# Narrower first weight loads and earlier transposes in the opening of a gated-MLP and long-convolution kernel

## The chip, the cores and the metric

The kernel runs on one core of a Trainium2 chip. The metric is the device time of one execution in microseconds; the median of three runs is given. A profiled execution is a run of its own, with its own time, and its trace covers a span that is a little shorter than that time.

## What is computed

The input `A_q` has 2048 rows of 640 columns. It is layer-normalised to `xn`, and two branches are added to it:

```python
xn  = layernorm(x)                                   # x = A_q, 2048 x 640
A   = xn * (causal long convolution of (shift_conv(k) * v) with ssm_k, plus D term)
B   = (sigmoid(xn @ w_gate) * (xn @ w_up)) @ w_down  # 640 -> 1728 -> 640
out = x + A + B
```

The change touches only the beginning of branch B: the first load of `x` and of the two weights, and the first products with them.

## The kernel before

**Layout.** The 2048 rows are 16 blocks of 128 (`b` in `x[:, b, :]`; row 16p+b lies on partition p). Four blocks make a tile `t` of 512 rows. For each tile `xn` is transposed block by block on TensorE (`xn_mm`, L230, five 128x128 transposes into `pt`), copied to `xnT` (`xn_ev`, L236; ScalarE's copy has L223), and multiplied with 128 columns of a weight at a time. Such a product is five matmuls of 512 columns (`product`, L253, matmuls at L257), one for each 128 of the 640 rows of the weight. ScalarE takes the sigmoid of the gate product (`gate_ev`, L266), and VectorE multiplies it with the up product into `hT` (`up_ev`, L272). The down product (L296) follows, and VectorE adds it to `x` (L301).

Both weights lie in one tile `w`, gate columns first, up columns from `UP` on. `load_w(eng, lo, hi, u)` loads columns lo to hi of gate (u = 0, DMA at L173) or up (u = 1, L176), as 5 chunks on 128 partitions.

**The opening.** Tile 0 starts before all its rows are there. For the first two column groups (fc = 0 and 1) its products are made in quarters: `quarter(u, fc, i)` (L242, matmuls at L248) multiplies one block of 128 rows. `turn(i)` (L484) transposes block i and copies it. The order on TensorE is 15 matmuls on zeros (`busy`, L482), turn 0, two more such matmuls, then block after block the four quarters gate 0, up 0, gate 1, up 1, with the turns in between: turn 1 after up 0 of block 0, turn 2 after up 0 of block 1, turn 3 after up 1 of block 1.

Behind each block of `x` stands a chain on VectorE: statistics (`ln_stats`, L198, two halves), aggregation (L202), variance (L210), then a power on GpSimd (L214) and the normalised block (`ln_xn`, L219). The chain of the next block is interleaved with it.

**What sets the order.** Everything is scheduled by hand. Each engine executes its instructions in the order in which the program issues them, and after the opening that order is the string ORDER (L621), one letter for each step. DMAs are issued from two queues only: SyncE's (SP) for nearly all of them, and ScalarE's (ACT) for three at the very beginning. In a queue they are issued in program order. After the loads shown in the diff, SyncE's queue goes on with the weight columns from 512 up, `w_down`, k (`load_k`, L155, first read by VectorE at L329), `ssm_k` (L139) and v (L169).

**Buffers.** The transposed blocks of tile 0 and `idle` share two PSUM buffers (`psC`), and the gate and up products have four (`psG`). A fifth product waits until the first of these is read: the first whole product takes the buffer that the sigmoid of gate 0 frees.

Of the kernel before, what the change touches and what calls it, by code (L numbers as in the profile page):

```python
# [19 lines left out]
P = 128  # L20
# [37 lines left out]
def kernel(  # L58
# [14 lines left out]
    nc = tc.nc  # L73
    xr = A_q.flatten_outer_dims().rearrange("(p b) d -> p b d", b=NB)
# [30 lines left out]
    x = res.tile([P, NB, DM], BF16, name="x")  # L105
# [15 lines left out]
    sync = nc.sync  # L121
# [49 lines left out]
    def load_w(eng, lo, hi, u):  # L171
        if u == 0:
            eng.dma_start(w[:, :, lo:hi], wgr[:, :, lo:hi])  # L173
            return
        h = min(hi, 13 * P)
        eng.dma_start(w[:, :, UP + lo:UP + h], wur[:, :, lo:h])  # L176
        if hi == FF:
            eng.dma_start(w[:, :, FF:UP], wur[:, :, h:FF])
# [51 lines left out]
    def xn_mm(g, i):  # L230
        pool, tag = (psG, "g") if g else (psC, "c")
        xts[i] = pt = pool.tile([P, NC, P], BF16, name="pt", tag=tag)
        for c in range(NC):
            nc.tensor.transpose(pt[:, c, :], xn[:, 4 * g + i, c * P:(c + 1) * P], ident[:])  # L234

    def xn_ev(g, i, copy=act_copy):  # L236
        copy(out=xnT[:, i, :, :], in_=xts[i][:, :, :])
# [4 lines left out]
    def quarter(u, fc, i):  # L242

        if i == 0:
            pgs[u, fc] = psG.tile([P, 512], F32, name=("pg", "pu")[u], tag="g")
        o = u * UP + fc * P
        for c in range(NC):
            nc.tensor.matmul(pgs[u, fc][:, i * P:(i + 1) * P], lhsT=w[:, c, o:o + P], rhs=xnT[:, i, c, :],  # L248
                             start=(c == 0), stop=(c == NC - 1))
# [216 lines left out]
        nc.vector.tensor_tensor(xs, xs, chunks[c]["yx", m][:, :, :], ALU.add)  # L466


    sync.dma_start(x[:, 0, :], xr[:, 0, :])
    nc.scalar.dma_start(x[:, 1, :], xr[:, 1, :])  # L470
    nc.scalar.dma_start(x[:, 2:4, :], xr[:, 2:4, :])
    for u in range(2):
        load_w((sync, nc.scalar)[u], 0, 256, u)
    for u in range(2):
        load_w(sync, 256, 512, u)

# [7 lines left out]
    def turn(i):  # L484
        xn_mm(0, i)
        xn_ev(0, i)
# [13 lines left out]
    for i in range(4):  # L500
        for fc in range(2):
            for u in range(2):
                quarter(u, fc, i)
            if (i, fc) in ((0, 0), (1, 0), (1, 1)):
                turn(1 + i + fc)
    for fc in range(2):
        gate_ev(0, fc)
        up_ev(0, fc)
# [158 lines left out]
```

## Time and profile before

| what | us |
|---|---|
| median of 3 runs (lowest, highest) | 239.71 (239.46, 240.14) |
| the profiled execution's own time | 239.41 |
| its span in the trace | 237.6 |
| TensorE (PE) busy | 231.4 |
| VectorE (DVE) busy | 190.3 |
| ScalarE (ACT) busy | 141.2 |
| first whole product (L257) starts | 14.34 |
| last matmuls end | 234.4 |
| x block 0, issue to landing | 3.2 |
| x blocks 2 and 3, issue to landing | 4.4 |
| first up load on ScalarE's queue, issue to landing | 7.1 |

All times inside the execution count from the start of the span. PE is the matmul part of TensorE and PEld its weight loads, which overlap with it; DVE is VectorE, ACT ScalarE, POOL GpSimd and SP SyncE. A matmul's shown length includes its way through the array, so that neighbours overlap: the distance from start to start is what one costs in a row of them. "Idle before <- releaser" names what ended a wait. A DMA's line shows its issue; its data come later, at its landing. The DMA view counts packets: one packet is one contiguous row piece, so a weight load of 256 columns (2 bytes each) has packets of 512 bytes and one of 128 columns has packets of 256.

### The profile page before, as it was taken

To read this page: it belongs to the slowest core of one execution; us is meant where nothing else is said; L and a number is where in the kernel's file an instruction comes from. 1 tells how busy PE (TensorE), PEld (TensorE's weight loads), DVE (VectorE), ACT (ScalarE), POOL (GpSimd) and SP (SyncE) were. 2 spreads that over 40 slices of the span, in tenths; PEclk is the share of its full clock that TensorE was granted. 3 is DMA by queue.
4 is the path that set the end of the run, shared out by engine and by line. 5 is a ranking of instruction groups with operands and counts; after the bars stand their busy time and mean duration, and the time that the engine had idled before them with its cause. 6 is when DMAs were issued, how large, how long until landed. Compare 5 with 4: busy or idle time off the path is not lost.

```text
span 237.6 us, 5553 instructions
## 1 busy us (share of the span) xinstructions
PE 231.4 (97%) x2265; PEld 135.1 (57%) x2265; DVE 190.3 (80%) x350; ACT 141.2 (59%) x178; POOL 11.2 (5%) x24
## 2 busy tenths in 40 slices
PE   8799999999999999999999999999999999999994
PEld 2564445878556455667754434577664434456782
DVE  3633889999999999999999999865585695968372
ACT  2342331728559897864888887997558858764000
POOL 4210000020000000002001000000000000000000
PEclk9999999999999999999999999999999999999999
DMA  7999999889998999999444888975939795285674
GB/s 212 292 314 233 259 322 298 183 249 284 253 311 243 253 295 297 284 267 319 148 183 152 234 230 258 227 228 203 241 109 222 186 281 123 89 238 144 196 237 134
DMA packets 88975, 54.82 MB, mean 231 GB/s; under 512 B 47670, under 2 KB 83062, under 8 KB 88694
## 3 DMA queue, kind: packets, MB, share of 16 engines
q1 hardware_dynamic: 88006, 53.66, 80.8%
q10 hardware_dynamic: 944, 0.82, 1.1%
q8 instruction: 17, 0.28, 0.5%
q14 instruction: 8, 0.07, 0.1%
HBM read 36.12 MB, written 18.35 MB: 229 GB/s over the span
## 4 chain that ended last, share of the span: by engine, by line
PE 95%; DMA 3%; ACT 0%; DVE 0%; ACTq 0%; issue 0%
PE pd L296 26%; PE pg L257 23%; PE pu L257 23%; PE psb L456 4%; PE ps L357 4%; PE ps L355 4%; PE ps L388 3%; DMA w<-in_B_w_up_dram 3%; PE psa L417 2%; PE pg L278 2%; PE pt L234 2%; PE pu L248 1%; PE pg L248 1%; ACT xnT L223 0%; DVE x L301 0%; ACT L119 0%
## 5 line engine op out<-in xcount | busy, mean ns | idle before, releaser
L257 PEld LDWEIGHTS <-w 128*128 128x128 bf16 x500 | 46.5, 98 | 54.3 <-issue 5.3
L296 PE MATMUL pd<-wd,hT 128*128 128x320 bf16 x448 | 64.3, 299 | 0.0
L257 PE MATMUL pg<-xnT,w 128*128 128x512 bf16 x250 | 62.2, 379 | 0.0
L257 PE MATMUL pu<-xnT,w 128*128 128x512 bf16 x250 | 62.1, 379 | 0.0
L296 PEld LDWEIGHTS <-hT 128*128 128x128 bf16 x448 | 42.8, 98 | 17.8 <-issue 1.7
L266 ACT ACTIVATE sig<-pg 128x512 bf16<-128x512 f32 x52 | 31.3, 605 | 30.1 <-PE pg L257 28.2
L272 DVE TENSOR_TENSOR hT<-sig,pu 128x512 bf16<-128x512 bf16 x52 | 35.2, 679 | 14.7 <-PE pu L257 9.3
L223 ACT CAST t<-ps 128x1024 bf16<-128x1024 f32 x40 | 39.1, 1023 | 11.4 <-DMA d<-t 6.3
L223 ACT CAST xz<-ps 128x1024 bf16<-128x1024 f32 x40 | 38.6, 1018 | 10.6 <-PE ps L388 10.5
L301 DVE TENSOR_TENSOR x<-pd,x 128x320 bf16<-128x320 f32 x32 | 15.4, 480 | 15.8 <-PE pd L296 15.7
L403 DVE TENSOR_TENSOR xz<-xz 128x2048 bf16<-128x2048 bf16 x20 | 24.4, 1220 | 0.2
L357 PE MATMUL ps<-kvh,S1t 128*128 128x128 bf16 x160 | 21.2, 219 | 0.0
L335 DVE TENSOR_TENSOR acc<-acc,tmp 128x1024 bf16<-128x1024 bf16 x30 | 20.7, 689 | 0.7
L355 PE MATMUL ps<-kvh,S1t 128*128 128x128 bf16 x160 | 21.2, 217 | 0.0
L333 DVE TENSOR_TENSOR tmp<-kx,sc 128x1024 bf16<-128x1024 bf16 x30 | 20.6, 687 | 0.4
L223 ACT CAST ao<-psa 128x1024 bf16<-128x1024 f32 x16 | 15.6, 1014 | 5.6 <-PE psa L417 3.5
L461 DVE TENSOR_TENSOR yx<-psb,xn 128x512 bf16<-128x512 f32 x20 | 13.8, 691 | 3.9 <-PE psb L456 2.9
L355 PEld LDWEIGHTS <-S1t 128*128 128x128 bf16 x160 | 15.5, 97 | 2.3
L357 PEld LDWEIGHTS <-S1t 128*128 128x128 bf16 x160 | 15.3, 96 | 2.3
L223 ACT COPY xnT<-pt 128x640 bf16<-128x640 bf16 x16 | 10.2, 709 | 10.8 <-PE pt L234 10.5
L198 DVE BATCH_NORM_STATS2 st<-x 128x6 f32<-128x320 bf16 x32 | 13.7, 471 | 2.8 <-DMA x<-in_A_q_dram 2.8
L401 DVE STREAM_SHUFFLE xz<-xz 128x512 f32<-128x512 f32 x20 | 14.6, 728 | 0.0
(44 smaller groups left out, 146.1 us busy)
## 6 DMA issues: line engine op xcount, KB each, us to landing
d<-t SPq DMA_DIRECT2D x20, 512.0 KB, 3.7
t<-d SPq DMA_DIRECT2D x20, 512.0 KB, 4.9
bi<-d SPq DMA_DIRECT2D x8, 512.0 KB, 5.5
d<-ao SPq DMA_DIRECT2D x6, 512.0 KB, 4.1
kx<-in_A_k_dram SPq DMA_DIRECT2D x10, 256.0 KB, 5.0
hn<-in_A_ssm_k_dram SPq DMA_DIRECT2D x20, 128.0 KB, 6.0
kvh<-in_A_v_dram SPq DMA_DIRECT2D x10, 256.0 KB, 5.2
x<-in_A_q_dram SPq DMA_DIRECT2D x3, 640.0 KB
```

Of the source, the lines that this page charges most:

```text
L223: nc.scalar.copy(out=out, in_=in_)
L257: nc.tensor.matmul(pg[:, :], lhsT=w[:, c, u * UP + fc * P:u * UP + (fc + 1) * P], rhs=xnT[:, :, c, :], start=(c == 0), stop=(c == NC - 1))
L266: nc.scalar.activation(sig[fc][:, :], pgs[0, fc][:, :], ACT.Sigmoid)
L272: nc.vector.tensor_tensor(hT[:, fc, :], sig[fc][:, :], pgs[1, fc][:, :], ALU.mult)
L296: nc.tensor.matmul(pd[:, :], lhsT=hT[:, fc, bb * P:(bb + 1) * P], rhs=wd[:, fc, 320 * half:320 * half + 320], start=(fc == 0), stop=(fc == ...
L301: nc.vector.tensor_tensor(x[:, 4 * t + bb, es], pds[bb, half][:, :], x[:, 4 * t + bb, es], ALU.add)
L333: nc.vector.tensor_tensor(d["tmp"][:, :, :], kx[:, lo + 3 - m:hi + 3 - m, :], sb(m), ALU.mult)
L335: nc.vector.tensor_tensor(d["acc"][:, :, :], d["acc"][:, :, :], d["tmp"][:, :, :], ALU.add)
L355: nc.tensor.matmul(ps[:, i, 0:P], lhsT=S1[:, b, h, :], rhs=cin[c]["kvh"][:, 0, b, :], start=True, stop=True)
L357: nc.tensor.matmul(ps[:, i, P:2 * P], lhsT=S1[:, b, h, :], rhs=hp[:, b // 2, b % 2, :], start=True, stop=True)
L401: nc.vector.stream_shuffle(z[:, 2, :, :].bitcast(F32), z[:, 1, :, :].bitcast(F32), swap)
L403: nc.vector.tensor_tensor(z[:, 1:3, :, :], z[:, 0:1, :, :].to_broadcast((P, 2, 8, P)), z[:, 1:3, :, :], ALU.mult)
```

## The change

```diff
-    sync.dma_start(x[:, 0, :], xr[:, 0, :])
-    nc.scalar.dma_start(x[:, 1, :], xr[:, 1, :])
-    nc.scalar.dma_start(x[:, 2:4, :], xr[:, 2:4, :])
-    for u in range(2):
-        load_w((sync, nc.scalar)[u], 0, 256, u)
+    for n in range(2):
+        for i in range(2):
+            (sync, nc.scalar)[i].dma_start(x[:, 2 * n + i, :], xr[:, 2 * n + i, :])
+        for u in range(2):
+            load_w((sync, nc.scalar)[u * (1 - n)], P * n, P * n + P, u)
     for u in range(2):
         load_w(sync, 256, 512, u)
...
         for fc in range(2):
             for u in range(2):
                 quarter(u, fc, i)
-            if (i, fc) in ((0, 0), (1, 0), (1, 1)):
-                turn(1 + i + fc)
+                if u + fc == 0 and i < 3:
+                    turn(i + 1)
```

The loads: columns 0 to 256 of both weights were one load of 320 KB each, gate on SyncE's queue, up on ScalarE's. Now they are four loads of 160 KB. Blocks 2 and 3 of `x`, one load of 320 KB on ScalarE's queue before, become two of 160 KB. The queues now carry, in order:

| queue | before | after |
|---|---|---|
| SP | x0, gate 0:256, gate 256:512, up 256:512, ... | x0, gate 0:128, x2, gate 128:256, up 128:256, gate 256:512, up 256:512, ... |
| ACT | x1, x2 and x3, up 0:256 | x1, up 0:128, x3 |

The turns: the turn of block i+1 now stands behind gate 0 of block i, for blocks 0, 1 and 2. The quarters keep their order, the instructions on the compute engines are the same in number and kind, and ORDER and everything after the opening stays as it is.

## The prediction

> **What bounds the kernel.** The first view is the busy time of each engine, and beside it the waits of the PE queue:
>
> ```profile
> PE 231.4 (97%) x2265; PEld 135.1 (57%) x2265; DVE 190.3 (80%) x350; ACT 141.2 (59%) x178; POOL 11.2 (5%) x24
> ```
> ```profile
> PE idle L482 <- DVE hT L117: 1.2, 1, 1.2
> PE pu L248 <- DMA w<-in_B_w_up_dram: 0.6, 1, 0.6
> PE pt L234 <- DVE xn L219: 0.6, 1, 0.6
> PE pg L248 <- ACT xnT L223: 0.6, 2, 0.3
> ```
>
> PE is busy for 231.4 of 237.6 us. All its waits that the second view names lie in the opening, before the loop over ORDER starts. The busy time by stage says the same (stretch in us, its length, then busy time of PE, PEld and so on, granted clock, DMA share, GB/s):
>
> ```profile
> 7.78:14.34 6.56, 5.74 (x95) 5.39 (x95) 2.31 (x10) 2.72 (x5) 1.74 (x3) 1.00 1.17 291
> 14.34:40.00 25.66, 25.66 (x125) 11.87 (x123) 18.49 (x28) 7.66 (x13) 0.42 (x1) 1.00 1.12 282
> 40.00:160.00 120.00, 120.00 (x1208) 72.70 (x1206) 115.24 (x213) 89.16 (x112) 5.41 (x7) 1.00 0.85 247
> 160.00:234.40 74.40, 74.36 (x823) 42.90 (x820) 49.80 (x89) 39.45 (x48) 0.00 (x0) 1.00 0.67 187
> ```
>
> From 14.34 us, the first whole product (L257), to 234.40 PE idles 0.04 us. So what the change does to the start of that product goes through to the end unless something that does not move with PE becomes late. The quarters' stage is the one to read, line by line in the timeline (start, length, engine, line; a bracket holds idle time and its releaser):
>
> ```profile
> 7.03 0.69 ACT L223 COPY xnT<-pt 128x640 bf16<-128x640 bf16 x1 [4.37 <-PE pt L234]
> 7.50 0.43 DVE L219 TENSOR_SCALAR xn<-x,mv,rstd 128x640 bf16<-128x640 bf16 x1
> 7.78 0.44 PE L248 MATMUL pg<-xnT,w 128*128 128x128 bf16 x5 [0.35 <-ACT xnT L223]
> 8.81 0.45 PE L248 MATMUL pu<-xnT,w 128*128 128x128 bf16 x5 [0.60 <-DMA w<-in_B_w_up_dram]
> 9.10 0.44 PE L234 MATMUL pt<-ident,xn 128*128 128x128 bf16 x5
> 9.58 0.69 ACT L223 COPY xnT<-pt 128x640 bf16<-128x640 bf16 x1 [1.85 <-PE pt L234]
> 10.32 0.44 PE L248 MATMUL pg<-xnT,w 128*128 128x128 bf16 x5 [0.22 <-ACT xnT L223]
> ```
>
> Groups of five matmuls follow one another every 0.28 us where nothing waits (12.10, 12.38, 12.66). From 7.78 to 14.34 stand 16 quarters and 3 turns: 19 x 0.28 = 5.32 of 6.56 us. The other 1.24 are waits, counted by starts: 8.06 to 8.81 for the up weights (0.75), 9.94 to 10.32 for xnT of block 1 (0.38), 12.00 to 12.10 for block 2 (0.10).
>
> **Part 1, the order on PE.** No instruction is added or removed on PE, ACT or DVE. A turn costs the group that needs it 1.22 us from its own start: 0.48 to the copy (9.10 to 9.58), 0.69 copy, 0.05 to the matmul (10.27 to 10.32); 10.88 to 12.10 is the same 1.22. Now the turn of block i+1 stands behind the first gate group of block i, and three other groups (0.84) follow it before block i+1 begins. Turn and cover make 1.12, so 0.10 stays as a wait, and one block takes 0.28 + 1.22 = 1.50 us. The first gate groups start at 7.78 (unchanged: xnT of block 0 sets it, and the chain of x block 0, its statistics and turn(0) is not touched), 9.28, 10.78 and 12.28. From the gate group of block 3 to the first product it is 1.13 now (13.21 to 14.34; sig of L266 frees the PSUM buffer at 14.29) and the four groups of block 3 keep their order, so that product starts at 13.41: **0.93 us earlier**.
>
> What is late next? The turns go up to xn. Turn 1 would stand at 8.06, and xn of block 1 is there at 7.93 + 0.05: 0.08 to spare. Turn 2 at 9.56 against 9.43, turn 3 at 11.06 against 10.85. What queues behind a turn that waits is every quarter after it. This holds if DVE's rows stay, so x blocks 2 and 3 must land by 6.71 and 8.16, where their statistics (L198) start, block 2 by 6.79 with the spare 0.08.
>
> **Part 2, the loads.** The trace has no 128-column weight load. Its price comes from the DMA view of two microseconds, the first (20 to 21 us) with loads of 256-byte rows of k, the second (8.2 to 9.2 us) with 512-byte rows of weights:
>
> ```profile
> DMA packets 857, 0.22 MB, mean 224 GB/s; under 512 B 848, under 2 KB 857, under 8 KB 857
> ```
> ```profile
> DMA packets 579, 0.29 MB, mean 289 GB/s; under 512 B 14, under 2 KB 579, under 8 KB 579
> ```
>
> A weight load is 640 packets (128 partitions, 5 chunks) whatever its width: 640/579 = 1.11 us at 256 columns, 640/857 = 0.75 at 128. Four narrow loads take 3.0 us of the DMA engines where two wide ones took 2.2: 0.2 more each. Lower end: half a wide load, nothing more. Upper end: a narrow packet as dear as a wide one, 0.55 more each. I take 0.2, the row of the same packet size.
>
> When do they land? The rates by microsecond (19, 212, 367, 372, 303, 293 GB/s from 1 to 7 us) add up to 970 kB at 5.0 us and 1273 kB at 6.0. Up to x block 2 the new order moves at most four blocks of x and two narrow loads, 983 kB (5.05 us); up to the second up load 1311 kB (6.1 us). Add 0.4 and 0.8 for small packets: 5.45 and 6.9. Then the lag to landing: x blocks 2 and 3 landed at 1.22 + 4.4 = 5.6 while their equal share of two queues was through at 5.05, 0.55; the up load on ScalarE's queue landed at 1.65 + 7.12 = 8.77 where that share says 7.25, 1.5. I take 0.55 for x (its own row) and keep both for the weights. Block 2 lands near **6.0** (needed 6.79), the second up load at **7.5 to 8.4** (its group now starts at 8.90, and 0.10 more is covered by the wait for xnT). The first up half has less ahead of it, and needs 8.34. So the 0.75 wait goes, and no DMA takes its place.
>
> The Trainium skill speaks against this change: "DMA: Bandwidth & Descriptors", Specifications, wants transfers of 512 bytes or more for line rate and says that shorter ones are read, modified and written. If that made a narrow packet as dear as a wide one, the gain would shrink to that of rival B. The trace agrees in direction only: 224 against 289 GB/s, not half.
>
> On SyncE's queue stand three more issues, 0.4 to 0.5 each. The waits of that queue name one for an x block, 0.3 before the ninth transfer (L176 at 4.17). In the new order the ninth is gate 256:512, so I let it move from 1.64 to about 4.2. With the slowest early landing, 7.1, it is there at 11.3; needed at 13.41. All loads behind come 0.8 later, PE 0.93 earlier. The tightest is k's first half (L155, issued 15.28, to landing 7.6, first read by L329 at 23.85): 0.97 to spare now, up to 0.8 late then. That sits on DVE, which idles 7.2 of 25.66 us in this stage, and a product's buffer has room: the multiply ending 17.46 frees what the product at 19.73 takes, 2.27 us. So I cost it at nothing; with the cover gone it is 0.8.
>
> **Sum.** -0.93 + 0 = -0.93 us. The profiled execution took 239.41 (span 237.6, 1.81 around it) and would take 238.48; it is 0.30 under the median of 239.71. On the median: **238.8 us**.
>
> **Rivals.**
> A, the forecast, 238.8 (own range 238.4 to 239.2). For it: PE's unbroken rows from 14.34. Chance 0.62.
> B, narrow packets cost as much as wide ones. Four cost 2.2 more: up lands at 6.1 + 2.2 + 0.55 to 1.5 = 8.9 to 9.8, so the last group of block 0 is late by 0 to 0.9 and 0.1 of it is covered. About 0.6 of the gain goes: -0.3, **239.4**. The 857 packets speak against it; that two queues of small packets are not in the trace speaks for it. Chance 0.17.
> C, PE starts earlier but gives it back: k's first half or another late load holds DVE (115.24 busy of 120 from 40 us on), and PE waits there for what it gained. **239.7**. The 2.27 us of buffer speak against it. Chance 0.12.
> D, slower: x block 2 now stands behind a weight load on SyncE's queue. If it lands after 6.79, statistics, xn and all turns slide by as much; from 7.72 on (0.93 late) the change loses. With the slowest early landing, 7.1 from an issue at 1.65, it lands at 8.75: 1.96 late, +1.03, **240.7**. Against it: with its own 160 KB SyncE's queue carries 480 KB up to its end, as much as ScalarE's queue carried up to the landing at 5.6. Chance 0.09.
>
> **Numbers.** 0.3% is 0.72 us, about what a measurement of this kernel can tell from no change. Faster by more (under 239.0): most of A and little else, 0.55. Slower by more (over 240.4): most of D, 0.07. Within: 0.38. The range takes in A, B and C, 238.3 to 239.8; it leaves out D and the lower tail of A.
>
> **What would show it.** Right: PE's waits no longer name the up weights; block 1 to 3 begin every 1.50 us with about 0.1 for xnT; the first L257 starts near 13.4; the last matmuls end 0.9 earlier. Wrong: a PE wait for w in block 0 (B); L198 waiting for x a second time (D); new PE waits behind 14 us (C), most likely for DVE. A start of turn(0) that moves by itself would upset every number here, as the sum stands on 7.78.

## The result and the profile after

The changed kernel takes 240.55 us (median of 22 runs, 239.11 to 243.03), the kernel before 239.66 (22 runs, 239.15 to 241.01). The ratio is 1.0034, with a 95% interval of 1.0018 to 1.0050: **0.8 us slower**, where 0.9 faster was forecast, and outside the range. The changed kernel also scatters more. The profiled execution took 240.36, its span is 238.3.

First the busy time and all the waits of the PE queue in the changed kernel:

```profile
PE 233.3 (98%) x2265; PEld 135.5 (57%) x2265; DVE 190.6 (80%) x350; ACT 140.9 (59%) x178; POOL 11.2 (5%) x24
```
```profile
PE idle L482 <- DVE hT L117: 1.2, 1, 1.2
PE pg L248 <- ACT xnT L223: 0.3, 1, 0.3
```

By this the change worked: the wait for the up weights is gone, and PE waits less than before. The stages say the same of the opening (columns as in the prediction):

```profile
8.43:14.05 5.62, 5.62 (x96) 5.43 (x96) 1.49 (x7) 2.73 (x5) 1.42 (x3) 1.00 1.17 290
40.00:160.00 120.00, 119.95 (x1201) 72.08 (x1200) 115.26 (x213) 88.34 (x111) 5.41 (x7) 1.00 0.87 248
```

From the first quarter (8.43) to the first product (14.05) it is 5.62 us, where 5.63 was forecast and 6.56 stood before. Yet the span is 0.7 us longer, and no wait tells why. Two things hide it.

**The start.** The timeline's line of the warm-up matmuls, before and after:

```profile
1.18 4.79 PE L482 MATMUL idle<-hT 128*128 128x512 bf16 x15 [1.18 <-DVE hT L117]
```
```profile
1.18 6.19 PE L482 MATMUL idle<-hT 128*128 128x512 bf16 x15 [1.18 <-DVE hT L117]
```

The same 15 matmuls take 1.4 us more. They follow one another every 0.43 us until about 4 us in the one execution and until about 7 us in the other; only then the trace's clock record begins with full speed. This is a matter of the execution, not of the change: over all traces of this study that moment lies between 3.9 and 7.1 us, in kernels with either opening. Here it moves the first quarter from 7.78 to 8.43, so that 0.29 of the 0.94 us is left at 14 us.

**The stretch at 53 us.** The same two groups in both timelines, the three transposes of the next tile and the down product behind them, before and then after:

```profile
53.29 1.00 PE L234 MATMUL pt<-ident,xn 128*128 128x128 bf16 x15
...
55.31 1.93 PE L296 MATMUL pd<-wd,hT 128*128 128x320 bf16 x13
```
```profile
53.04 1.17 PE L234 MATMUL pt<-ident,xn 128*128 128x128 bf16 x15
...
55.50 1.79 PE L296 MATMUL pd<-wd,hT 128*128 128x320 bf16 x12
```

The first pair is 2.02 us apart, the second 2.46. PE comes 0.25 ahead (0.29 just before) and leaves 0.19 behind. No wait is listed: the loss comes in five steps of 0.04 to 0.14 us, and the shown length of a group of transposes overlaps the next one by 0.16 (0.44 long, 0.28 apart). What PE waits for shows on the other engines.

The names in the next lines: the convolution works in chunks of 128 channels. For each chunk, `sraw` holds the taps of shift_k, which ScalarE copies to `sc` (L151), and `hn` holds ssm_k, which VectorE rearranges into `kvh` (L315). `S1t` is a table for PE's products of all chunks (L355, L357). ScalarE copies their results into `t`, and a store (L369) writes `t` to `d` in DRAM and so frees `t` for a later copy. The longest waits from 30 to 60 us in the queues of SyncE and ScalarE before:

```profile
SPq L159 <- DMA S1t<-tabS: 3.0, 1, 3.0
```
```profile
ACT t L223 <- DMA d<-t: 4.4, 1, 4.4
```

and after, with VectorE's:

```profile
SPq L159 <- DMA S1t<-tabS: 4.9, 1, 4.9
...
SPq L369 <- DMA hn<-in_A_ssm_k_dram: 0.9, 1, 0.9
```
```profile
ACT t L223 <- DMA d<-t: 5.3, 1, 5.3
ACT sc L151 <- DMA sraw<-in_A_shift_k_dram: 2.4, 1, 2.4
```
```profile
DVE kvh L315 <- DMA hn<-in_A_ssm_k_dram: 0.3, 1, 0.3
```

All these are loads, or a store that stands behind a load in SyncE's queue. ScalarE and VectorE now wait for loads themselves (taps, ssm_k), which they did not before. ScalarE's taps, S1t and ssm_k (`hn`) are, but for the `x` rows of the next tile, the last of the loads that keep this queue full from 3 to 42 us; only for some 2 us, from 21 us before and from 22 after, does the DMA share fall to 0.7 or 0.8, so that the engines that move the data have room. SyncE's issues of S1t and of the store, and ScalarE's copies that wait for this store, before:

```profile
30.35 0.57 SPq L635 DMA_DIRECT2D S1t<-tabS  x1
...
46.53 0.38 SPq L369 DMA_DIRECT2D d<-t  x1
```
```profile
52.25 1.93 ACT L223 CAST t<-ps 128x1024 bf16<-128x1024 f32 x2 [4.37 <-DMA d<-t]
54.07 2.50 ACT L223 COPY xnT<-pt 128x640 bf16<-128x640 bf16 x4
```

and after:

```profile
31.12 0.57 SPq L635 DMA_DIRECT2D S1t<-tabS  x1
...
47.61 0.38 SPq L369 DMA_DIRECT2D d<-t  x1
```
```profile
52.92 1.93 ACT L223 CAST t<-ps 128x1024 bf16<-128x1024 f32 x2 [5.33 <-DMA d<-t]
54.74 2.50 ACT L223 COPY xnT<-pt 128x640 bf16<-128x640 bf16 x4
```

The issue of S1t moved from 30.35 to 31.12, 0.8 later, as forecast. A transfer's landing is counted in sixteen parts; fifteen of S1t's came 0.9 later, but the last, which a waiting queue needs too, landed at 41.5 in place of 39.8. The queue stood still for it, and the store that frees ScalarE's buffer left at 47.61 in place of 46.53. The remaining 0.36 us went at 77 and 124 us, at ScalarE's copies that wait for other stores of this kind.

### The profile page after: what moved, and what is told of

Read it like the earlier page. It is cut to its first block, busy times and chain, and to the rows that moved or that the text cites. A ratio compares the mean times of both kernels' runs of the same rounds, so it can differ in the third digit from the quotient of the medians.

```text
span 238.3 us, 5556 instructions
## 1 busy us (share of the span) xinstructions
PE 233.3 (98%) x2265; PEld 135.5 (57%) x2265; DVE 190.6 (80%) x350; ACT 140.9 (59%) x178; POOL 11.2 (5%) x24
## 4 chain that ended last, share of the span: by engine, by line
PE 97%; ACT 1%; DVE 0%; issue 0%; ACTq 0%
PE pd L296 26%; PE pu L257 23%; PE pg L257 23%; PE ps L355 4%; PE psb L456 4%; PE ps L357 4%; PE ps L388 3%; PE idle L482 3%; PE psa L417 3%; PE pt L234 2%; PE pg L278 2%; PE pg L248 1%; PE pu L248 1%; ACT t L223 0%; ACT xnT L223 0%; DVE x L301 0%
## 5 line engine op out<-in xcount | busy, mean ns | idle before, releaser
L296 PEld LDWEIGHTS <-hT 128*128 128x128 bf16 x448 | 42.9, 98 | 17.9 <-issue 1.7
L355 PE MATMUL ps<-kvh,S1t 128*128 128x128 bf16 x160 | 21.2, 217 | 0.0
L357 PE MATMUL ps<-kvh,S1t 128*128 128x128 bf16 x160 | 21.2, 219 | 0.0
L223 ACT CAST ao<-psa 128x1024 bf16<-128x1024 f32 x16 | 15.6, 1014 | 6.3 <-PE psa L417 4.3
L357 PEld LDWEIGHTS <-S1t 128*128 128x128 bf16 x160 | 15.4, 96 | 2.6 <-issue 0.3
L355 PEld LDWEIGHTS <-S1t 128*128 128x128 bf16 x160 | 15.5, 97 | 2.3
```

Source lines behind the costliest of these rows:

```text
L223: nc.scalar.copy(out=out, in_=in_)
L296: nc.tensor.matmul(pd[:, :], lhsT=hT[:, fc, bb * P:(bb + 1) * P], rhs=wd[:, fc, 320 * half:320 * half + 320], start=(fc == 0), stop=(fc == ...
L355: nc.tensor.matmul(ps[:, i, 0:P], lhsT=S1[:, b, h, :], rhs=cin[c]["kvh"][:, 0, b, :], start=True, stop=True)
L357: nc.tensor.matmul(ps[:, i, P:2 * P], lhsT=S1[:, b, h, :], rhs=hp[:, b // 2, b % 2, :], start=True, stop=True)
```

## The experiments

**Theory 1, the stream**: the narrow loads make every later load of SyncE's full queue late; the engines wait for the last of them at 42 to 55 us, and PE gives back there what it gained and more. **Theory 2, the opening alone**: what the opening gains reaches the end, and only the late clock spoiled it. **Theory 3**: the new place of the turns costs something itself. Each kernel was run in turns with the kernel before; ratios are to that one.

The table comes from the timelines, one profiled execution each. Its first four columns are starts in us (L315 is VectorE's first step on the ssm_k of the second chunk, counted as chunk 1; the copy is the one that waits for the store). The last four tell how much later than in the profile of before the same matmul of PE starts, near 44, 56, 80 and 234 us.

| kernel | first quarter | first product | VectorE L315 of chunk 1 | ScalarE copy at 52 us | 44 | 56 | 80 | 234 |
|---|---|---|---|---|---|---|---|---|
| before | 7.78 | 14.34 | 43.98 | 52.25 | 0 | 0 | 0 | 0 |
| changed | 8.43 | 14.05 | 44.11 | 52.92 | -0.29 | 0.19 | 0.39 | 0.55 |
| e1 turns only | 7.51 | 14.28 | 43.91 | 50.96 | -0.06 | -0.06 | -0.06 | -0.14 |
| e2 loads only | 7.87 | 13.66 | 43.49 | 51.81 | -0.68 | -0.68 | -0.68 | -0.75 |
| e3 wide | 8.36 | 13.98 | 43.62 | 51.46 | -0.36 | -0.36 | -0.36 | -0.28 |
| e4 narrow later, twice | 7.41 | 14.21 | 44.54 | 53.96 | -0.13 | 1.23 | 1.53 | 1.46 |
| e5 store first | 7.42 | 13.04 | 44.23 | 49.17 | -1.30 | 0.04 | 1.32 | 1.44 |
| e6 before, store first | 8.54 | 14.33 | 43.97 | 48.95 | -0.01 | -0.01 | 1.20 | 1.24 |
| e7 narrow later, once | 7.77 | 14.15 | 43.78 | 51.66 | -0.19 | -0.19 | -0.19 | -0.04 |
| e8 wide, 12 warm-ups | 7.45 | 13.45 | 43.09 | 51.33 | -0.89 | -0.88 | -0.88 | -0.95 |
| e9 changed, light | 7.48 | 13.10 | 42.73 | 47.84 | -1.24 | -1.24 | -1.24 | -1.31 |
| e10 before, light | 8.24 | 14.56 | 44.19 | 49.36 | 0.22 | 0.22 | 0.22 | 0.15 |
| e11 before, 12 warm-ups | 7.46 | 14.60 | 44.23 | 50.78 | 0.26 | 0.26 | 0.26 | 0.29 |
| e12 changed, 12 warm-ups | 7.53 | 13.15 | 44.10 | 53.40 | -1.19 | 0.66 | 0.98 | 0.91 |

### The parts of the change

**e1_turns_only**, the kernel before with this:

```diff
-            if (i, fc) in ((0, 0), (1, 0), (1, 1)):
-                turn(1 + i + fc)
+                if u + fc == 0 and i < 3:
+                    turn(i + 1)
```

> Loads as before, turns as in the changed kernel. Theory 1 (the stream): SyncE's queue is full from 3 to 42 us, so its transfers keep their absolute times whatever PE does, and at 52 to 55 us ScalarE's copies wait for a store that follows in this queue (4.4 us of waiting at L223 in the profile of before); PE has 0.48 us to spare there. The opening gains 0.56 (the up load still lands at 8.8, the rest as predicted), and about 0.5 of it reaches the end: 239.2. Theory 2 (the opening alone): what the opening gains or loses reaches the end, and the changed kernel lost only because its warm-up matmuls ran at the low clock until 6.8 us: 0.56 faster, 239.1. Theory 3 (the new place of the turns costs something of its own): slower than before.

Measured: 239.05, ratio 0.9980 (0.9964 to 0.9996). The turns alone gain some 0.5 us. Theory 3 falls.

**e2_loads_only**, the loads of the change with the turns of before:

> Loads as in the changed kernel, turns as before. Theory 1: the opening gains 0.75 (no wait for the up weights), but all later loads come 0.8 to 1.0 later, the load of S1t too, behind whose landing SyncE's queue stands at about 40 us (3.0 us before, 4.9 in the changed kernel). So as slow as the changed kernel: 240.2 to 240.6, and the store of d before 52 us is issued some 1 us later than before. Theory 2: 0.75 faster, 239.0. Theory 3: as theory 2, the slowness goes with the turns.

Measured: 240.40, ratio 1.0034 (1.0010 to 1.0059), the changed kernel's own ratio. The loads carry the whole loss. The profiled execution (238.81) was the fastest of the twelve and lost nothing at 55 us, so its line in the table shows what the opening gains when nothing is given back: 0.68 to 0.75, as expected by both theories.

**e3_wide**, the changed kernel with 256-column loads:

```diff
-        for u in range(2):
-            load_w((sync, nc.scalar)[u * (1 - n)], P * n, P * n + P, u)
+        for u in range(2 - 2 * n):
+            load_w((sync, nc.scalar)[u], 0, 256, u)
```

> The changed kernel with 256-column loads (gate on SyncE's queue, up on ScalarE's, each between two x blocks): same turns, same split of x, no narrow packets. Theory 1: opening as in the changed kernel (5.6 us from the first quarter to the first product), stream as in before: about 0.5 faster than before, 239.2, no more, for the spare at 55 us is 0.48. Theory 2: no different from the changed kernel in the opening, so 0.9 faster or as slow as it, by the clock. Theory 3: as slow as the changed kernel, 240.4.

Measured: 239.12, ratio 0.9987 (0.9968 to 1.0005). The interval just takes in no change, but lies wholly below that of the loads alone. The same turns, the same split of x, and the opening as short (5.62 us): without narrow packets the loss is gone.

### The dose

**e4_narrow_later**: the opening of before; four wide loads that nobody waits for become eight narrow ones.

```diff
     def load_w(eng, lo, hi, u):
+        if hi - lo == 256 and lo in (512, 768):
+            for a in (lo, lo + P):
+                eng.dma_start(w[:, :, u * UP + a:u * UP + a + P], (wgr, wur)[u][:, :, a:a + P])
+            return
```

> Opening as before; the four weight loads of columns 512 to 1024 are split into eight of 128 columns, which are needed 6 us or more after they land. That is twice the extra packets of the change, some 1.6 us of the DMA engines, with no effect on the opening. Theory 1: the stream is 1.6 us late at 40 us, less the 0.48 to spare: about 1 us slower, 240.7, first lost by PE at 53 to 55 us. Theories 2 and 3: as before, 239.7.

Measured: 241.29, ratio 1.0067 (1.0046 to 1.0088): 1.6 us, where 1 was expected. Waits of VectorE in this kernel (its lines stand 4 further down), the second and third of which the kernel before doesn't have:

```profile
DVE st L202 <- DMA x<-in_A_q_dram: 2.5, 1, 2.5
DVE kvh L319 <- DMA hn<-in_A_ssm_k_dram: 0.6, 1, 0.6
DVE acc L333 <- DMA kx<-in_A_k_dram: 0.3, 1, 0.3
```

PE loses 1.36 us between 44 and 56. Nothing of the opening was touched, so theory 2 falls for the loss.

**e7_narrow_once**: half the dose (`lo == 512`), the extra packets of the change.

> Opening as before; only the two loads of columns 512 to 768 are split, into four of 128 columns: the same extra packets as in the change (0.8 us), with no gain in the opening. Twice that lost 1.6 us. Theory 1 with a spare of 0.48: 0.3 to 0.4 slower, 239.8. If the loss goes with the dose: 0.8 slower, 240.3. No loss would speak against the stream as the cause in the changed kernel.

Measured: 240.35, ratio 1.0030 (1.0006 to 1.0055): 0.7 us. The loss goes with the dose; a spare of 0.48, as I had it from one profile, doesn't show in the mean. This kernel's profiled execution (239.51) was again among its fastest and lost nothing at 55 us. So the loss is not the same in every execution, and the spare that one profile shows is that execution's.

Two narrow loads in place of a wide one are also one transfer more, and no run here adds transfers without small packets. But the trace of this kernel has the narrow loads alone from 9 to 10 us:

```profile
DMA packets 875, 0.22 MB, mean 219 GB/s; under 512 B 875, under 2 KB 875, under 8 KB 875
```

2560 packets at 875 per us, less 1280 at the 579 that the wide loads showed, make 0.72 us; S1t was issued 0.70 later (31.05), and fifteen of its parts landed 0.79 later. The packets alone account for the delay.

What this does to the landings shows in all traces with the full stream. The last part of S1t landed at 37.5 to 39.8 us in the six kernels with wide loads and at 40.7 to 41.5 in the six with narrow ones; that of the second chunk's ssm_k at 41.7 to 42.9 and at 43.4 to 44.3.

### Which of the late loads

**e5_store_first**, the changed kernel with ORDER edited, so that the first store and the ssm_k load of the third chunk go ahead of v and taps:

```diff
-...mutmkm
-    auTaAHgAHDagAwlhauaAl...
+...mutk
+    auaAHgAHDagAwlhmmTauaAl...
```

> The changed kernel with the first store of d (L369) and the next load of ssm_k put ahead of the second chunk's v loads and taps in SyncE's queue; the loads and the turns of the change stay. Theory 1 in its narrow form: the change is slow because SyncE's queue stands behind the landing of S1t and so issues that store late (47.6 in the changed kernel, 46.5 before), and ScalarE's copies at 52 us wait for it. Then the store goes at about 45.6, ScalarE's copy starts near 51, PE loses at most 0.4 at 53 to 55 us, by VectorE's chain alone: 0.2 to 0.4 faster than the kernel before, 239.1 to 239.3, over 1 us faster than the changed kernel. Theory 1 in its wide form (any of the stream's late loads, ssm_k for VectorE above all, would do it): 0.3 to 0.8 slower than before, little better than the changed kernel.

Measured: 239.97, ratio 1.0018 (1.0003 to 1.0034). This lies where the wide form put it and misses the 239.1 to 239.3 of the narrow form, but e6 below shows that the reordering has a price of its own. In the profiled execution (240.98, among the slower of the twelve) the store left at 44.5 and ScalarE's copy started at 49.2, 3 us early; the opening was even 1.3 us ahead, and still all of it went at 53 us, to VectorE. Its wait, and behind it PE's in the timeline:

```profile
DVE kvh L315 <- DMA hn<-in_A_ssm_k_dram: 1.5, 1, 1.5
```
```profile
53.16 1.17 PE L234 MATMUL pt<-ident,xn 128*128 128x128 bf16 x15 [0.94 <-DVE xn L219]
```

VectorE's L315 starts at 44.23, 0.25 later than before, whatever PE gained. From there to the normalised blocks (L219) VectorE has no idle time in which it could catch up. The time of that load's landing is what PE meets at 53 us.

**e6_before_store_first**: the same edit of ORDER in the kernel before.

> The same reordering of SyncE's queue in the kernel before. It tells what the reordering brings without the change. Narrow form: before has 0.48 us to spare at that place in its profile, so within 0.3 of it: 239.3 to 239.5. If it gains more than that, most executions of the kernel before lose there too.

Measured: 240.63, ratio 1.0037 (1.0012 to 1.0063). The reordering itself costs, at 74 to 77 us (1.21 us between 56 and 80 in the table; e5 pays 1.28 there). So e5 has to be held against e6 and not against the kernel before, and by that it is 0.7 us faster, where the change without the reordering is 0.8 slower. The runs of the two overlap, so that a gain isn't shown. But with the store out of the way the loss isn't there: this speaks for the store's part, and the narrow form is not refuted. What the trace of e5 adds is VectorE's line, which takes PE's lead without the store's help.

### Relief of the queue

**e9_light_after** and **e10_light_before**: both kernels without the load of the second half of `w_down`, 1040 KB of the stream. The down products use the rows of the first half twice, so that part of the result is other data.

```diff
-            nc.tensor.matmul(..., rhs=wd[:, fc, 320 * half:320 * half + 320],
+            nc.tensor.matmul(..., rhs=wd[:, fc % 7, 320 * half:320 * half + 320],
...
-              (load_wd, sync, 7, NFC),
```

> The changed kernel without the load of the second half of w_down (1040 KB); the down products take the first half's rows twice, so that part of the result is other data. All later loads of SyncE's queue come some 3 us earlier, the taps, S1t and ssm_k that are late in the changed kernel among them. Theory 1 (the change loses because these loads come later in a full queue, and whatever PE gains in the opening is given back where VectorE or ScalarE waits for them at 42 to 55 us): with the queue relieved the opening's 0.9 us reach the end, 0.8 to 1.0 faster than the same kernel with the opening of before: 238.4 to 238.7. Rival (the narrow loads or the turns cost something that has nothing to do with those loads, or the loss lies in the stores after 70 us): still 0.3% slower than its twin, 240.1.

> The kernel before without the load of the second half of w_down, as its twin. Theory 1: before has little to gain at 42 to 55 us, 0 to 0.4 faster: 239.2 to 239.6. If it gains a microsecond, the kernel before too is held back by this queue in most executions.

Measured: 238.48, ratio 0.9961 (0.9937 to 0.9984), and 239.43, ratio 0.9989 (0.9973 to 1.0004). With room in the queue the change is worth 0.95 us between the medians (nine of e9's eleven runs lie under the lowest of e10), and for the kernel before no gain from the room is shown. From 30 to 60 us VectorE has one wait left in e9, for PE and not for a load:

```profile
DVE hT L272 <- PE pu L257: 0.9, 1, 0.9
```

### The warm-up

**e8_wide_busy12** (e3 with `busy(12)` in place of `busy(15)`), **e11_before_busy12** and **e12_after_busy12** (the same in the kernel before and in the changed one):

> Wide loads, new turns, and 12 warm-up matmuls in place of 15. In the profiles the clock was granted between 3.9 and 6.8 us, and where it came late the 15 matmuls ended at 7.4 in place of 6.0 and the first quarter started at 8.4 in place of 7.5 to 7.8. Twelve end at 6.4 even at the low clock, before the first normalised block is there. If that start reaches the end: 0.2 to 0.4 faster than with 15 in the mean, 238.8, and less spread. If SyncE's stream sets the time at 55 us: no different from 15, 239.1.

> The kernel before with 12 warm-up matmuls in place of 15. In three of ten profiles the clock was granted at 6.7 us or later and the first quarter started 0.6 to 1.0 us late behind the slow warm-up matmuls. Without that: 0.2 to 0.3 faster in the mean, 239.4, with less spread, as far as the stream at 42 to 55 us lets it through. The wide loads gained 0.5 by the same edit.

> The changed kernel with 12 warm-up matmuls. Theory 1: the late loads set the time at 42 to 55 us, an earlier opening is given back there: no gain on the changed kernel, 240.2 to 240.6. Theory 2 (what the opening gains reaches the end): 0.3 to 0.5 faster than the changed kernel, 240.0.

Measured: e8 238.57, ratio 0.9957 (0.9941 to 0.9972), the fastest kernel of the study that computes everything (five runs). With wide loads an earlier start reaches the end, by more than the 0.2 to 0.4 expected over e3's 239.12: in the table it is 0.89 ahead at 44 us and 0.95 at 234. e11 239.37, ratio 0.9997 (0.9977 to 1.0016): no gain shown. In its profile the first quarter starts early (7.46), and PE then waits longer for the up weights:

```profile
PE pu L248 <- DMA w<-in_B_w_up_dram: 1.2, 1, 1.2
```

In the opening of before the up load's landing swallows an early start as well as a late one. e12: 240.52, ratio 1.0029 (1.0010 to 1.0047), as slow as the changed kernel. Its opening is among the best of the study (13.15, 1.19 ahead at 44 us), and at 53 to 56 us it loses 1.85. The waits of VectorE, ScalarE and PE there:

```profile
DVE kvh L315 <- DMA hn<-in_A_ssm_k_dram: 1.2, 1, 1.2
```
```profile
ACT t L223 <- DMA d<-t: 6.7, 1, 6.7
ACT sc L151 <- DMA sraw<-in_A_shift_k_dram: 3.2, 1, 3.2
```
```profile
PE pt L234 <- DVE xn L219: 0.8, 1, 0.8
PE ps L355 <- ACT t L223: 0.3, 1, 0.3
```

The three loads don't care when PE arrives: L315 starts at 44.11 in the changed kernel and at 44.10 here, though PE came 0.9 earlier, and the last parts of taps and ssm_k landed at 41.9 and 44.0 in both. That is theory 1 in two lines.

## Why the prediction was wrong

- **The order on PE** was right: 5.62 us from the first quarter to the first product (5.63 forecast), about 0.1 of waiting per turn. With the queue relieved the change gains 0.95 (0.93 forecast).
- **The loads of the opening** were right: no PE wait for weights, x block 2 in time, so rivals B and D did not occur. A narrow load cost about what the 256-byte rows of k gave: S1t was issued 0.8 later after four of them.
- **Where it failed: "All loads behind come 0.8 later ... The tightest is k's first half ... So I cost it at nothing."** The 0.8 was right for the issues and for fifteen parts in sixteen (S1t: 0.77 and 0.86), but a reader waits for the last part, and that came 1.7 later for S1t, 1.3 for the taps and 1.1 for ssm_k. And k was not where it counts. Its first half had 1.4 to spare (it took 7.2 us; the 7.6 is the second half's), 0.2 was left in the changed kernel, and it cost nothing. I looked for the tightest among the first loads that VectorE reads. But a delay in this queue passes to the last loads in it, and these cannot take the change: taps and ssm_k are read at 42 to 44 us, 1.25 and 1.09 after they landed in the trace of before, and the queue itself waits for S1t. There the sum needed 0.8 of lateness plus 0.93 of PE's lead against the landing of the second ssm_k load (last part 42.9, read at 43.98 in the trace of before): 1.1 to spare against 1.7. The same goes for the store behind S1t in the queue: ScalarE's copy waited 4.4 us for it even before; in the changed kernel the store landed 0.68 later and the copy started 0.67 later, and PE has 0.48 to spare behind it. Neither place was priced; both stand in the trace of before, in the waits of SyncE's queue for S1t and of ScalarE's for the store.
- **Rival C** had the mechanism, with chance 0.12 and a bound that was wrong: "gives it back" is not the end of it. The time at 53 us is set by the landings. If they come 0.8 later than before, PE ends up behind its old time, and its gain doesn't enter at all. The cover that I named, PSUM buffers, sits at the gate and up products; the loss came in at the transposes of the next tile, for which VectorE works without a pause, and at ScalarE's copies of them.
- **The sum stood on 7.78**, as the text said. The clock's late start moved it by 0.65 in the profiled execution. In the kernel before such a shift is absorbed by the wait for up weights, in the changed one it is not.
- **The Trainium skill's rule** ("DMA: Bandwidth & Descriptors", Specifications: 512 bytes or more for line rate) spoke against the change. I weighed it only for the opening, where the trace agreed that it would not decide. It decided 30 us later, through the queue, at 219 GB/s against 289: by 0.7 us for 2560 packets of 256 bytes in place of 1280 of 512 (e7), 1.6 for twice as many (e4).
- **How the loss divides at 53 us** can be read from the traces, one execution each. VectorE's normalised blocks (L219) are 0.14 late in the changed kernel and in e12, 0.27 in e5 and 0.59 in e4. The last of the three transposes at 53 us stands 0.22 to 0.23 better than that, 0.09 and 0.08 ahead, 0.04 and 0.36 behind. ScalarE's copies of the transposed blocks, which follow the copies that wait for the store, are 0.67, 1.15 and 1.71 late in the changed kernel, e12 and e4, and PE's down product at 55.3 us is 0.19, 0.67 and 1.23 late, each time 0.48 less. In e5, where the store came early, nothing is added. So VectorE's way (ssm_k, L315) takes PE's lead away, and ScalarE's way (the store behind S1t) sets how far behind PE ends.

What stays open is why the last parts come so much later than the rest, and by how much in each execution. The losses at 74 to 77 and 124 us follow landings of stores and were not tested.

## What to carry to other kernels

In a queue that is full for a long time, price a few tenths of added transfer at the last load of the full stretch, not at the first, and compare the landing of its last part with where its reader will stand after the gain. An engine's gain reaches only as far as the next point where everything waits for something that keeps its own time. And compare start-to-start distances of the same instructions: 0.48 us went here without one listed wait on PE.

## What the runs showed of the hardware

- The sixteen parts in which a transfer's landing is counted do not end together, and where the queue carried narrow loads the last of S1t's lagged longer: 2.3 to 2.8 us behind the fifteenth in the six traces with them, 0.2 to 2.0 in the six without. In the trace of before, fifteen parts of S1t had landed by 37.8 us and the last at 39.8; of the second ssm_k load by 40.8 and at 42.9. At 36.85 us a 16 KB instruction fetch (queue q8 of the page) ran for 1.1 us; after the fetches at 15.6 and 52.3 us, too, the last parts of several transfers came 0.9 to 1.4 later than the rest, and elsewhere mostly 0.04 to 0.3. In the trace of before the coincidence is clear, but not everywhere: behind the fetch at 50.3 us in e3's no part lags by more than 0.3. The cause was not tested. The Trainium skill ("DMA: Bandwidth & Descriptors", Why a DMA increments its semaphore by 16 and not by 1) says that only the full count means that all data are there; the trace agrees, as VectorE started L315 at 44.11, behind the last part at 44.03 and not behind the fifteenth at 41.9.
- SyncE's queue waits for an earlier transfer before it issues one that reuses its semaphore: k of the second chunk (L159) waited 3.0 to 4.9 us for S1t, which it doesn't read; both count on one semaphore (100 before, 106 in the changed kernel). Such a wait stops everything behind it, stores included.
- The matmul clock rose between 3.9 and 7.1 us from execution to execution, with the same warm-up matmuls before it.
